# Five small edits to a block-sorted attention and cosine-gated MLP kernel: where one output tile, two transposes and the last columns live, and when one transpose and two value products run

## The chip, the cores and the metric

The kernel runs on one core of a Trainium2 chip. The core has a matrix engine (PE, with its weight loads listed apart as PEld), a vector engine (DVE), a scalar engine (ACT), a GpSimd engine (POOL) and a sync engine (SP), each with its own in-order instruction queue, and 16 DMA engines that all queues share. Matrix products land in PSUM, a small memory of eight banks per partition; DVE and ACT copy from there to SBUF, and DMAs move SBUF to and from device memory. The metric is the device time of one execution in microseconds (us); lower is better.

## The reference

```python
# attention: 4 batches x 8 heads, 768 tokens of 64, 8 blocks of 96 tokens
P = sort_net
for _ in range(5):
    P = exp(P - max(P, -1))
    P = P / (sum(P, -1) + 1e-9)
    P = P / (sum(P, -2) + 1e-9)
k_sorted = einsum('bhij,bhjcd->bhicd', P, k_blocks)
v_sorted = einsum('bhij,bhjcd->bhicd', P, v_blocks)
attn = softmax(q_block @ k_sorted_block.T / sqrt(64))
x = attn @ v_sorted_block            # -> 3072 tokens x 512
# MLP
h = x @ w_in                         # 512 -> 2048
out = (h * cos(h)) @ w_out           # 2048 -> 512, float32
```

Every query block of 96 tokens attends to one block of keys, which is a mixture of all eight key blocks of its head; the result goes through an MLP whose gate is the cosine of its own input.

## The kernel before

**Chunks.** The 3072 tokens are cut into eight chunks, n = 0 to 7, of four blocks (u = 0 to 3) of 96 tokens: 384 tokens, or three output tiles of 128 tokens (ts = 0 to 2). For each chunk the kernel makes scores (`qk`, `qk_half`; in the first two chunks `s_ps`, `s_max`, `s_sub`), exponentials on ACT (`expo`), the transpose of the exponentials (a DMA that SP issues, or PE products with an identity), the value products with their normalisation on DVE (`av` is `av_products` and then `av_norm`), and the transpose of the normalised tokens into `xT` (a DMA that SP issues, or `x_transpose` on PE with a copy from PSUM). The MLP follows: `up` makes two of sixteen column blocks of h in PSUM, ACT takes their cosine into a tile `c`, DVE multiplies both into `gg`; `down` sums sixteen products of 512 columns per output tile, in two halves of eight, and copies the sum to SBUF for the store.

**Order.** Nothing schedules the work: each engine runs its instructions in the order in which the program writes them (`manual_schedule`). A `moe_down` call takes lists of attention steps for a later chunk: list e runs after the e-th of six halves (`slots`), and `mid={e: ...}` runs between the fourth and the fifth product of half e. So the attention of chunk n + 1 is threaded by hand through the MLP of chunk n. An instruction that waits holds all that is written behind it on its engine.

**Buffers.** A tile pool hands out its buffers in turn; a new tile waits until the readers of the buffer's previous tile are done. The pools that matter here:

```python
cosp = ctx.enter_context(tc.tile_pool(name="cosp", bufs=2))
op = ctx.enter_context(tc.tile_pool(name="op", bufs=2))
big = ctx.enter_context(tc.tile_pool(name="big", bufs=3, space=bass.MemoryType.PSUM))
acc = ctx.enter_context(tc.tile_pool(name="acc", bufs=2, space=bass.MemoryType.PSUM))
```

`big` has three PSUM buffers of two banks and `acc` two of one bank; the program calls them `B` and `C` (line 618). `cosp` holds the cosines and `op` the output tiles in SBUF that wait for their store. From chunk 3 on most output tiles go to parts of the old value buffer instead (`vbuf`, the first half of the tile `kv`), six places of 512 float32 columns, and are stored one chunk later (`let_go`).

**The places that the change and the prediction touch.**

- End of chunk 0 and of the attention of chunk 1 (lines 940 to 984): `down_out(2, A)` (line 950) copies chunk 0's third output tile by ACT to an `op` buffer; its two buffers were taken by the other two output tiles. Behind it ACT copies one token transpose and four products of the key mixing (`kse` for 3, 2, 1 and 0; the fifth, 5, is DVE's). Then come `k_swap(kT[1])` (line 968, two DMAs on SP that bring key halves to the other partitions, behind the last of the `kse`), the query transposes `q_transpose(2, 0)` and `(2, 1)` (969, 970; sixteen PE products each, placed by DVE), `up(1, 0)` (977), two groups of value mixing (`v_sort_b`), `up(1, 1)`, and `qk_half(2, 0, 0)` (984), the first products that read the swapped keys.
- End of chunk 1 (lines 1021 to 1027): value products of chunk 2 and its token transposes `x_transpose(2, u)`, each into a `big` buffer, among the halves of the third output tile.
- `moe_down(3)` (line 1060): the last list runs `av(4, 3)`, `expo(5, 0)`, the transpose of tokens of blocks 1 and 2 together, and `qk(5, 1)`.
- `moe_down(6)` (line 1088): `av(7, 2)` behind the third half, `av(7, 3)` behind the fourth.
- The tail (lines 1095 to 1109): the last output tile in two halves of 256 columns, each with sixteen products into `acc`; the second half is copied by DVE and ACT, 128 columns each, into one `op` tile, and stored by two DMAs, of SP and of ACT.

Of the kernel before, what the change touches and what calls it, by code (L numbers as in the profile page):

```python
# [10 lines left out]
FP32 = mybir.dt.float32  # L11
# [7 lines left out]
def kernel(  # L19
# [15 lines left out]
    nc = tc.nc  # L35
    B, H, S, D = q.shape
# [3 lines left out]
    Ntok, Dm = out.shape  # L40
# [9 lines left out]
    TC = IC * blk  # L50
    KC = Dm // 128
    FC = Dff // 128
# [8 lines left out]
    cosp = ctx.enter_context(tc.tile_pool(name="cosp", bufs=2))  # L61
    gp = ctx.enter_context(tc.tile_pool(name="gp", bufs=5))
    op = ctx.enter_context(tc.tile_pool(name="op", bufs=2))
    ctx.enter_context(tc.manual_schedule())

    big = ctx.enter_context(tc.tile_pool(name="big", bufs=3, space=bass.MemoryType.PSUM))
    acc = ctx.enter_context(tc.tile_pool(name="acc", bufs=2, space=bass.MemoryType.PSUM))

    kv = const.tile([128, 2 * CD], BF16, name="kv")
    vbuf, kbuf = kv[:, :CD], kv[:, CD:]  # L70
# [11 lines left out]
                      in_=sort_net.rearrange("b h i j -> (b h) (i j)"))  # L82
# [71 lines left out]
    w_out_t = const.tile([128, FC, Dm], BF16, name="w_out_t")  # L154
# [90 lines left out]
    V, A = nc.vector, nc.scalar  # L245

    def copy_on(eng, dst, src):
        if eng is nc.scalar:
            eng.copy(dst, src)  # L249
        else:  # L250
            eng.tensor_copy(dst, src)
# [3 lines left out]
    def q_products(n, z, lo, hi, pool, tag):  # L255
        if lo == 0:
            q_ps[n, z] = pool.tile([128, 2, IC, QR, blk // QR], BF16, name="qps", tag=tag)
        for i in range(lo, hi):
            e, hp, r = i // (2 * QR), i // QR % 2, i % QR
            nc.tensor.transpose(  # L260
                q_ps[n, z][hp * D:(hp + 1) * D, e, :, r],
                q_rows[:, (z * 2 + e) * 2 + hp, r * D:(r + 1) * D], ident[:blk, :blk])

    def q_transpose(n, z, engs, pool, tag):
        q_products(n, z, 0, 4 * QR, pool, tag)
        for hp, eng in enumerate(engs):
            q_place_half(n, z, hp, eng)

    def q_place_half(n, z, hp, eng):
        rows = slice(hp * D, (hp + 1) * D)  # L270
        dst = q_of(n, hp)[rows, :QW].rearrange("d (i h c) -> d h i c", h=H2, c=blk)
        copy_on(eng, dst[:, z * 2:z * 2 + 2],
                q_ps[n, z][rows].rearrange("d e i r p -> d e i (r p)"))
# [263 lines left out]
    def x_transpose(n, u, eng, pool, tag, to=None):  # L537
        us = range(u, (u if to is None else to) + 1)
        ps = pool.tile([128, KC, len(us), blk], BF16, name="xps", tag=tag)

        turn = order[:] if n < NQ else ident[:blk, :blk]
        for i, z in enumerate(us):
            xn = xn_t.pop((n, z))
            for h2 in range(H2):
                nc.tensor.transpose(  # L545
                    ps[:, h2, i], xn[:, h2].rearrange("p e d -> p (e d)"), turn)
        copy_on(eng, xT[n][:, :, u * blk:us.stop * blk], ps.rearrange("p k i c -> p k (i c)"))

    gt = {}
# [21 lines left out]
    def store(n, ts, o_s, eng=nc.sync):  # L571
        r0 = n * TC + ts * 128
        eng.dma_start(out=out[r0:r0 + 128, :], in_=o_s[:])
# [4 lines left out]
    def down(n, ts, half, stores, mid=()):  # L578
        if half == 0:
            out_ps[ts] = acc.tile([128, Dm], FP32, name="o", tag="acc")  # L580
        o = out_ps[ts]
        for f in range(half * FC // 2, (half + 1) * FC // 2):
            nc.tensor.matmul(  # L583
                o[:], gt[n, f // 4][:, f % 4, ts * 128:(ts + 1) * 128], w_out_t[:, f, :],
                start=(f == 0), stop=(f == FC - 1))
            if f % (FC // 2) == FC // 4 - 1:
                step(mid)
        if half == 0:
            return
        if stores is None:  # L590

            z = (n % 2 * 3 + ts) * 2 * Dm
            o_s = vbuf[:, z:z + 2 * Dm].bitcast(FP32)
        else:
            o_s = op.tile([128, Dm], FP32, name="o_s", tag="o_s")
        late = n > 0 and ts == TC // 128 - 1
        copy_on(V if late else A, o_s[:], o[:])
        if stores is None or stores == "held":
            kept[n, ts] = o_s
        else:  # L600
            store(n, ts, o_s, nc.sync if late else stores)

    def step(calls):
        for f, *args in calls:
            f(*args)
# [6 lines left out]
    def moe_down(n, slots=(), stores=nc.sync, mid={}):  # L612

        for e in range(2 * TC // 128):
            down(n, e // 2, e % 2, stores, mid.get(e, ()))
            step(slots[e] if e < len(slots) else ())

    B, C = (big, "big"), (acc, "acc")
# [139 lines left out]
                start=(f == 0), stop=(f == FC - 1))  # L758

    def down_out(ts, eng):  # L760
        o_s = op.tile([128, Dm], FP32, name="o_s", tag="o_s")
        copy_on(eng, o_s[:], out_ps[ts][:])
        store(0, ts, o_s)

# [201 lines left out]
    kse(5, V)  # L966
    kse(0, A)
    k_swap(kT[1])
    q_transpose(2, 0, (V, V), *B)
    q_transpose(2, 1, (V, V), *B)  # L970
    zeros_between(3)
    load_q(3)
# [50 lines left out]
    av(2, 2, True)  # L1023
    x_transpose(2, 1, V, *B)
    av(2, 3, True)
    x_transpose(2, 0, V, *B)
    down(1, 2, 1, nc.sync, mid=[(k_sort_g, 20, A, *B), (x_transpose, 2, 2, V, *B), (x_transpose, 2, 3, V, *B)])
    q_transpose_dma(4)
    moe_up(2, [[(k_next,), (qk_half, 3, 0, 0)], [(k_next,)],
# [4 lines left out]
    def ahead(n, *more):  # L1034
# [5 lines left out]
        for e, calls in more:  # L1040
# [8 lines left out]
             mid={5: [(x_transpose, 3, 1, V, *B), (x_transpose, 3, 2, V, *B),  # L1049
                  (x_transpose, 3, 3, V, *B)]})  # L1050
# [9 lines left out]
    moe_down(3, [[(qk, 4, 3), (expo, 4, 2)], [(w_next, A, *B), (qk, 5, 0), (expo, 4, 3)],  # L1060
                 [(av, 4, 0)],
                 [(av, 4, 1, True), (av, 4, 2, True)],
                 [(av, 4, 3, True), (expo, 5, 0), (x_transpose, 4, 1, A, *B, 2), (qk, 5, 1)]],
             None, mid={5: [(x_transpose, 4, 3, A, *B)]})

    q_transpose_dma(6)
# [8 lines left out]
             None, mid={3: [(av, 5, 1)], 5: [(x_transpose, 5, 3, A, *B)]})  # L1075
# [7 lines left out]
             mid={5: [(x_transpose, 6, 3, A, *B)]})  # L1083
# [1 line left out]
               [(qk_half, 7, 3, 1)]])  # L1085
    expo(7, 2)
    expo(7, 3)
    moe_down(6, [[(av, 7, 0)], [(av, 7, 1)], [(av, 7, 2, True)], [(av, 7, 3, True)],
                 [(x_transpose, 7, 2, A, *B)]], None,
             mid={5: [(x_transpose, 7, 3, A, *B)]})  # L1090
    moe_up(7, [[(let_go, 6, 0)], [(let_go, 6, 1)], [(let_go, 6, 2)]])
    for e in range(2 * TC // 128 - 2):
        down(7, e // 2, e % 2, nc.sync)

    ts, w = TC // 128 - 1, Dm // 2
    for z in range(2):
        o = acc.tile([128, w], FP32, name="o", tag="acc")
        for f in range(FC):
            nc.tensor.matmul(
                o[:], gt[7, f // 4][:, f % 4, ts * 128:(ts + 1) * 128],  # L1100
                w_out_t[:, f, z * w:(z + 1) * w], start=(f == 0), stop=(f == FC - 1))
        o_s = op.tile([128, w], FP32, name="o_s", tag="o_s")
        for e, (eng, dma) in enumerate((((A, nc.scalar),), ((V, nc.sync), (A, nc.scalar)))[z]):
            c = slice(e * w // 2, (e + 1) * w // 2) if z else slice(0, w)
            copy_on(eng, o_s[:, c], o[:, c])
            dma.dma_start(
                out=out[7 * TC + ts * 128:8 * TC, z * w:(z + 1) * w][:, c], in_=o_s[:, c])

# [1 line left out]
_INS = ['q', 'k', 'v', 'sort_net', 'moe_w_in', 'moe_w_out']  # L1110
# [26 lines left out]
```

## Time and profile before

| | |
|---|---|
| median of three runs | 241.41 us (241.0 to 241.5) |
| the profiled execution's own time | 240.86 us |
| its span, first to last instruction | 239.1 us |
| granted TensorE clock over the span | 1.000 |
| PE busy / weight loads busy | 227.4 us / 143.9 us |
| DVE / ACT / POOL busy | 171.1 / 153.9 / 93.6 us |
| bytes moved by DMA, mean rate | 30.89 MB, 129 GB/s |

The profiled execution is 0.55 us shorter than the median; between its span and its time lie 1.76 us. How to read the lines below: a row of the timeline has the start in us, the length, the engine, the line in the program, the operation with output <- input, shapes, a count where neighbouring rows were merged, and in brackets how long the engine stood idle before it and what seemed to end that. PE products overlap in the pipeline, so a row's length includes about 0.17 us of drain that the next row does not wait for. In the chain of waits the overlap is taken out: its lengths add up. "DMA to landing" is the time from the issue of a DMA on its queue until its semaphore tells that the data is there.

### The profile page before, as it was taken

The numbers are of one execution on the slowest core, as the hardware profiler recorded it, in microseconds if no ns is written. First come the engines' busy times: TensorE is split into PE (matmuls) and PEld (weight loads), VectorE is DVE, ScalarE is ACT, GpSimd is POOL, SyncE is SP. The second block draws the span as 40 slices with busy tenths as digits, with TensorE's granted clock in tenths as the row PEclk, the third lists the DMA queues.
The fourth block names the chain that finished last, engine by engine and source line by source line (L and its number), as shares of the span: only waits on it lengthen the run. The fifth ranks groups of instructions, "written<-read, shape, count | busy, mean of one in ns | idle before, by whom it ended". The sixth has DMA issues, their size and how long they took to land.

```text
span 239.1 us, 5377 instructions
## 1 busy us (share of the span) xinstructions
PE 227.4 (95%) x2191; PEld 143.9 (60%) x2214; DVE 171.1 (72%) x284; ACT 153.9 (64%) x205; POOL 93.6 (39%) x117
## 2 busy tenths in 40 slices
PE   8789999998999989999999989999999999999993
PEld 2468799566765656656666556655565565455552
DVE  5658976886789666893689966998698869535700
ACT  3357966586889747896688737674666477546511
POOL 7689994893970098930808005300000000000000
PEclk9999999999999999999999999999999999999999
DMA  6999999895899989769889959934973450341012
GB/s 87 210 201 204 205 221 216 142 194 159 102 108 190 144 154 140 141 154 187 102 93 109 122 103 238 79 60 88 127 205 57 84 174 3 66 121 47 0 44 88
DMA packets 66423, 30.89 MB, mean 129 GB/s; under 512 B 55136, under 2 KB 61920, under 8 KB 66144
## 3 DMA queue, kind: packets, MB, share of 16 engines
q0 software_dynamic: 24048, 13.64, 41.7%
q1 hardware_dynamic: 42064, 16.73, 32.8%
q8 instruction: 17, 0.28, 0.5%
q10 hardware_dynamic: 288, 0.20, 0.3%
q14 instruction: 6, 0.05, 0.1%
HBM read 27.27 MB, written 6.29 MB: 140 GB/s over the span
## 4 chain that ended last, share of the span: by engine, by line
PE 81%; DMA 6%; ACT 5%; DVE 3%; issue 3%; POOL 1%; SPq 0%; ACTq 0%; POOLq 0%
PE h L558 31%; PE o L583 22%; PE h L735 4%; PE o L756 4%; PE sc L405 3%; DMA pT<-p_buf 3%; PE av L514 3%; PE vs L662 2%; PE ks L375 2%; PE vs L425 1%; ACT p_buf L467 1%; DMA vperm<-p_buf 1%; PE pps L713 1%; DMA xT<-xn 1%; PE xps L545 1%
## 5 line engine op out<-in xcount | busy, mean ns | idle before, releaser
L558 PE MATMUL h<-xT,w_in_t 128*128 128x384 bf16 x448 | 78.4, 326 | 0.2 <-DMA xT<-xn 0.2
L583 PE MATMUL o<-w_out_t,gg 128*128 128x512 bf16 x303 | 73.6, 379 | 0.9
L566 DVE TENSOR_TENSOR gg<-c,h 128x768 bf16<-128x768 f32 x56 | 52.6, 949 | 19.0 <-ACT c L562 19.0
L562 ACT ACTIVATE c<-h,half_pi 128x768 f32<-128x768 f32 x56 | 50.4, 900 | 22.2 <-PE h L558 21.3
L558 PEld LDWEIGHTS <-w_in_t 128*128 128x128 bf16 x448 | 42.2, 98 | 26.5 <-issue 0.6
L583 PEld LDWEIGHTS <-gg 128*128 128x128 bf16 x320 | 29.1, 98 | 27.6
L179 POOL COPY vperm<-kv 64x1536 bf16<-64x1536 bf16 (+1 forms) x10 | 28.0, 2849 | 1.1 <-DMA kv<-in_v_dram 1.1
L467 ACT ACTIVATE p_buf<-s 96x768 bf16<-96x768 f32 x32 | 26.0, 840 | 3.0 <-DVE s L702 2.4
L449 DVE TENSOR_TENSOR s<-sc,mx 96x384 f32<-96x384 f32 (+1 forms) x33 | 24.3, 735 | 1.8
L447 DVE TENSOR_REDUCE mx<-sc 96x4 f32<-96x384 f32 (+1 forms) x33 | 24.0, 728 | 0.7 <-PE sc L405 0.7
L527 DVE TENSOR_TENSOR xn<-av,r 96x512 bf16<-96x512 f32 x32 | 22.0, 686 | 1.1
L525 DVE RECIPROCAL r<-av 96x8 f32<-96x8 f32 x32 | 6.3, 198 | 14.8 <-PE av L514 14.6
L129 POOL DMA_DIRECT2D kv<-in_q_dram x24 | 16.0, 681 | 0.8 <-issue 0.8
L405 PE MATMUL sc<-kTs,q_turned 128*128 128x96 bf16 x224 | 15.3, 206 | 0.0
L249 ACT CAST kTs<-ks 128x512 bf16<-128x512 f32 (+1 forms) x18 | 10.9, 637 | 6.4 <-PE ks L375 6.4
L405 PEld LDWEIGHTS <-q_turned 128*128 128x128 bf16 x224 | 12.7, 98 | 3.8 <-DVE s L449 0.4
L249 ACT COPY kv<-o 128x512 f32<-128x512 f32 x8 | 4.7, 582 | 12.8 <-PE o L583 12.8
L249 ACT COPY o_s<-o 128x512 f32<-128x512 f32 (+2 forms) x10 | 5.3, 532 | 10.7 <-PE o L583 6.4
L756 PE MATMUL o<-w_out_t,gg 128*128 128x512 bf16 x45 | 11.2, 380 | 0.2
L129 POOL DMA_DIRECT2D q_mem<-in_q_dram x16 | 10.7, 691 | 1.3 <-DMA kv<-in_v_dram 1.0
L735 PE MATMUL h<-xT,w_in_t 128*128 128x192 bf16 x128 | 11.1, 246 | 0.0
L238 PE MATMUL idle<-warm 128*128 128x512 bf16 x28 | 8.7, 450 | 2.4 <-ACT q_turned L321 1.4
(118 smaller groups left out, 282.8 us busy)
## 6 DMA issues: line engine op xcount, KB each, us to landing
out_dram<-kv SPq DMA_DIRECT2D x12, 256.0 KB, 2.5
out_dram<-o_s SPq DMA_DIRECT2D x11, 256.0 KB, 3.2
w_in_t<-in_moe_w_in_dram POOLq DMA_DIRECT2D x4, 512.0 KB, 12.2
w_out_t<-in_moe_w_out_dram POOLq DMA_DIRECT2D x4, 512.0 KB, 12.8
kv<-in_k_dram POOLq DMA_DIRECT2D x2, 768.0 KB, 10.2
kv<-in_v_dram POOLq DMA_DIRECT2D x2, 768.0 KB, 13.3
pair<-in_k_dram POOLq DMA_DIRECT2D x2, 768.0 KB, 11.3
kv<-in_v_dram POOLq DMA_DIRECT2D x6, 256.0 KB, 5.4
```

Of the source, the lines that this page charges most:

```text
L129: nc.gpsimd.dma_start(out=q_heads[:, i, :, e], in_=src[:, ih * IC + i, :, e])
L179: nc.gpsimd.tensor_copy(dst, src)
L249: eng.copy(dst, src)
L405: nc.tensor.matmul(out, q_of(n, hp)[:, x:x + 128], keys_of(n, u, h2, hp), start=True, stop=True)
L447: nc.vector.reduce_max(mx[:], scv, axis=AX.X)
L449: nc.vector.tensor_tensor(s, scv, mx.to_broadcast(list(s.shape)), op=ALU.subtract)
L467: nc.scalar.activation(p[:, :, :blk], s_t.pop((n, u)).rearrange("p e h c -> p (e h) c"), AF.Exp, scale=scale)
L527: nc.vector.tensor_tensor(xn.rearrange("p h e d -> p e h d"), avv[:, :, :, :D], r.to_broadcast([blk, 2, H2, D]), op=ALU.mult)
L558: nc.tensor.matmul(h[:, f2, :w], w_in_t[:, kk, f * 128:(f + 1) * 128], xT[n][:, kk], start=(kk == 0), stop=(kk == KC - 1))
L562: nc.scalar.activation(c[:], h[:, :, :w], AF.Sin, bias=half_pi[:, 0:1])
L566: nc.vector.tensor_tensor(gt[n, fp // 2][:, f:f + 2], c[:], h[:, :, :w], op=ALU.mult)
L583: nc.tensor.matmul(o[:], gt[n, f // 4][:, f % 4, ts * 128:(ts + 1) * 128], w_out_t[:, f, :], start=(f == 0), stop=(f == FC - 1))
```

## The change

1. `down_out`: the third output tile of chunk 0 goes to a buffer of the cosine pool, of which it uses 512 of 768 columns, instead of an `op` buffer.
2. `q_transpose(2, 0)` and `x_transpose(2, 0)` take `acc` buffers instead of `big` buffers.
3. `moe_down(3)`, last list: the transpose of blocks 1 and 2 comes first, then `expo(5, 0)`, then `av(4, 3)`, then `qk(5, 1)`.
4. `moe_down(6)`: `av(7, 2)` runs in the middle of the fourth half instead of ahead of it.
5. The tail: the last columns are 256, 128 and 128, each with its own `big` tile; the two tiles of 128 take turns, product by product. The copies go to the last place of `vbuf` instead of `op` tiles.

```diff
     def down_out(ts, eng):
-        o_s = op.tile([128, Dm], FP32, name="o_s", tag="o_s")
+        if ts < 2:
+            o_s = op.tile([128, Dm], FP32, name="o_s", tag="o_s")
+        else:
+            o_s = cosp.tile([128, 2, TC], FP32, name="c", tag="c")
+            o_s = o_s.rearrange("p b c -> p (b c)")[:, :Dm]
         copy_on(eng, o_s[:], out_ps[ts][:])
         store(0, ts, o_s)
...
-    q_transpose(2, 0, (V, V), *B)
+    q_transpose(2, 0, (V, V), *C)
     q_transpose(2, 1, (V, V), *B)
...
-    x_transpose(2, 0, V, *B)
+    x_transpose(2, 0, V, *C)
...
-                 [(av, 4, 3, True), (expo, 5, 0), (x_transpose, 4, 1, A, *B, 2), (qk, 5, 1)]],
+                 [(x_transpose, 4, 1, A, *B, 2), (expo, 5, 0), (av, 4, 3, True), (qk, 5, 1)]],
...
-    moe_down(6, [[(av, 7, 0)], [(av, 7, 1)], [(av, 7, 2, True)], [(av, 7, 3, True)],
+    moe_down(6, [[(av, 7, 0)], [(av, 7, 1)], [], [(av, 7, 3, True)],
                  [(x_transpose, 7, 2, A, *B)]], None,
-             mid={5: [(x_transpose, 7, 3, A, *B)]})
+             mid={3: [(av, 7, 2, True)], 5: [(x_transpose, 7, 3, A, *B)]})
...
-    ts, w = TC // 128 - 1, Dm // 2
-    for z in range(2):
-        o = acc.tile([128, w], FP32, name="o", tag="acc")
+    ts = TC // 128 - 1
+    for parts in (((0, 256, A, nc.scalar),), ((256, 128, V, nc.sync), (384, 128, A, nc.scalar))):
+        tiles = [big.tile([128, w], FP32, name="o", tag="big") for _, w, *_ in parts]
         for f in range(FC):
-            nc.tensor.matmul(
-                o[:], gt[7, f // 4][:, f % 4, ts * 128:(ts + 1) * 128],
-                w_out_t[:, f, z * w:(z + 1) * w], start=(f == 0), stop=(f == FC - 1))
-        o_s = op.tile([128, w], FP32, name="o_s", tag="o_s")
-        for e, (eng, dma) in enumerate((((A, nc.scalar),), ((V, nc.sync), (A, nc.scalar)))[z]):
-            c = slice(e * w // 2, (e + 1) * w // 2) if z else slice(0, w)
-            copy_on(eng, o_s[:, c], o[:, c])
-            dma.dma_start(
-                out=out[7 * TC + ts * 128:8 * TC, z * w:(z + 1) * w][:, c], in_=o_s[:, c])
+            for o, (c, w, *_) in zip(tiles, parts):
+                nc.tensor.matmul(
+                    o[:], gt[7, f // 4][:, f % 4, ts * 128:(ts + 1) * 128],
+                    w_out_t[:, f, c:c + w], start=(f == 0), stop=(f == FC - 1))
+        for o, (c, w, eng, dma) in zip(tiles, parts):
+            o_s = vbuf[:, (5 * Dm + c) * 2:(5 * Dm + c + w) * 2].bitcast(FP32)
+            copy_on(eng, o_s, o[:])
+            dma.dma_start(out=out[7 * TC + ts * 128:8 * TC, c:c + w], in_=o_s)
```

What it does to the instructions, at three places on ACT. The rows are the engine's instructions in order, with the semaphores each waits for: PE, DVE, Activation and Pool are the engines' own, DMAHW and DMASW those of DMAs issued by hardware queues and by POOL.

The first is the end of chunk 0, where ACT copies the third output tile (`o_1078`); the `xT` and `kTs` copies behind it belong to chunk 1's tokens and to the key mixing.

```order
 L249 COPY xT_1035<-xps_1109 128x4x96 [waits PE_49]
 L249 COPY pT_1095<-pps_1114 96x768 [waits PE_49]
-L249 COPY o_s_1155<-o_1078 128x512 [waits DMAHW1_49,PE_49,Activation_49]
+L249 COPY c_1155<-o_1078 128x512 [waits PE_49]
 L249 COPY xT_1035<-xps_1158 128x4x96 [waits PE_49]
 L249 COPY kTs_98<-ks_1167 128x2x32x8 [waits PE_49]
```

The copy keeps its place and no longer waits for a DMA.

The second is the last list of `moe_down(3)`: the copy of the joint token transpose of chunk 4 (`xps`, 192 columns) and the exponential of chunk 5's first block (`p_buf2_108`).

```order
 L467 ACTIVATE p_buf1_107<-s_2347 96x8x96 [waits DMAHW4_49,DVE_49]
 L249 COPY kv_87<-o_2394 128x512 [waits DMASW5_49,PE_49]
+L249 COPY xT_2403<-xps_2462 128x4x192 [waits PE_49]
 L467 ACTIVATE p_buf2_108<-s_2378 96x8x96 [waits DMAHW5_49,DVE_49]
-L249 COPY xT_2403<-xps_2477 128x4x192 [waits PE_49]
 L249 COPY xT_2403<-xps_2504 128x4x96 [waits PE_49]
 L562 ACT_TABLE_LOAD
```

The copy moved ahead of the exponential; on PE its eight products moved ahead of the value products of `av(4, 3)` in the same way.

The third is ACT's end: the copies of the last 256 and 128 columns and their DMAs.

```order
 L249 COPY o_s_3474<-o_3457 128x512 [waits PE_49]
 L249 COPY o_s_3494<-o_3477 128x512 [waits PE_49]
-L249 COPY o_s_3514<-o_3497 128x256 [waits DMAHW5_49,PE_49,Activation_49]
-L1106 DMA out_0_dram<-o_s_3514 128x256 [waits DMAHW7_49,Activation_49]
-L249 COPY o_s_3534<-o_3517 128x128 [waits DMAHW6_49,DVE_49]
-L1106 DMA out_0_dram<-o_s_3534 128x128 [waits DMAHW1_49,Activation_49]
-L1132 UNCONDITIONAL_BRANCH
+L249 COPY kv_87<-o_3497 128x256 [waits DMAHW5_49,DMASW6_49,PE_49]
+L1110 DMA out_0_dram<-kv_87 128x256 [waits DMAHW7_49,Activation_49]
+L249 COPY kv_87<-o_3517 128x128 [waits PE_49]
+L1110 DMA out_0_dram<-kv_87 128x128 [waits DMAHW0_49,Activation_49]
```

The last copy waited for DVE, which copies the other half of the same tile, and for a DMA; it now waits for PE alone.

## The prediction

> **What bounds the kernel now.** I read the page first.
>
> ```profile
> span 239.1 us, 5377 instructions
> PE 227.4 (95%) x2191; PEld 143.9 (60%) x2214; DVE 171.1 (72%) x284; ACT 153.9 (64%) x205; POOL 93.6 (39%) x117
> PE 81%; DMA 6%; ACT 5%; DVE 3%; issue 3%; POOL 1%; SPq 0%; ACTq 0%; POOLq 0%
> ```
>
> PE is busy nearly throughout, and four fifths of the chain that ends last are its products. The change adds none but sixteen small ones at the end, so it can only win where PE stands still. I therefore read the timeline and the chain at the five places of the change.
>
> **Place 1, end of chunk 0.** The rows are the timeline's; the three last lines are landing times, of the store issued at 49.21 (it carries the first `op` buffer), of the two key-swap DMAs here, and of the next such pair, at 100.32 and 100.84.
>
> ```profile
> 49.21 9.13 SPq L573 DMA_DIRECT2D out_dram<-o_s  x3
> 55.32 0.80 ACT L249 COPY pT<-pps 96x768 bf16<-96x768 bf16 x1
> 55.53 0.86 PE o L756 x4
> 56.92 0.69 DVE L527 TENSOR_TENSOR xn<-av,r 96x512 bf16<-96x512 f32 x1
> 57.40 0.58 ACT L249 COPY o_s<-o 128x512 f32<-128x512 f32 x1 [1.28 <-PE xps L722]
> 58.04 0.39 PE L375 MATMUL ks<-bd,kv 128*128 128x64 bf16 x8 [0.70 <-ACT o_s L249]
> 58.25 2.08 ACT L249 CAST kTs<-ks 128x512 bf16<-128x512 f32 x4
> 59.89 0.88 PE L260 MATMUL qps<-ident,q_mem 96*64 96x96 bf16 x32 [0.30 <-ACT kTs L249]
> 60.94 0.59 SPq L389 DMA_DIRECT2D kTs<-kTs  x1
> 64.12 0.33 PE L405 MATMUL sc<-kTs,q_turned 128*128 128x96 bf16 x4
> DMA to landing us min/median/max: 8.1/8.1/8.1
> 60.47 2.31 DVE L251 COPY q_turned<-qps 64x768 bf16<-64x768 bf16 x4 [0.44 <-PE qps L260]
> DMA to landing us min/median/max: 2.8/2.9/3.0
> DMA to landing us min/median/max: 3.7/4.4/5.0
> ```
>
> ACT's copy of the third tile could start when its sum is done, 55.53 + 0.86 = 56.39, and ACT is free from 56.12. It starts at 57.40. The row blames PE's `xps`, but the copy also waits for a DMA, and the store lands at 49.21 + 8.1 = 57.31: that is the wait. Behind it on ACT stand the four `kTs` casts, and PE waits for these twice (0.70, 0.30).
>
> With a cosine buffer the copy starts at about 56.42, 0.98 earlier. The ACT queue follows if its inputs come in time. The fourth is the tightest: its products need the token transpose after DVE's `xn` (56.92 + 0.69 = 57.61), then DVE's copy of that transpose (to about 58.40) and the last eight products (0.39 in the row at 58.04, done at 58.85), so the last cast ends near 59.40 instead of 60.33. The swap DMAs wait for it: the second goes out at 60.01 instead of 60.94 and lands at 60.01 + 3.0 = 63.01 instead of 63.94. The scores that read it start at about 63.07 instead of 64.12: **1.05 us**.
>
> The query turn in the other pool removes PE's wait of 0.30 for a cast, and lets the two turns run while casts are still going on. With both edits PE reaches `up(1, 0)` 1.24 us earlier, but then waits about 0.2 at the scores for the swap. The turn alone, without the first edit, would win almost nothing for that reason; I give it nothing of its own. It adds a wait: the second `v_sort_b` now needs DVE's placing of that turn. Four placings take 2.31; the two of this turn, behind DVE's last cast (to 59.2 by the same steps), end at 60.4, and PE gets there at 61.1. Cover 0.7. Bounds of the sum of both: 1.24 if the swap lands a little sooner; 0.1 if it takes a microsecond more (the next pair took up to 5.0).
>
> **Place 2, chunk 2's token transpose.**
>
> ```profile
> 85.96 0.69 DVE L527 TENSOR_TENSOR xn<-av,r 96x512 bf16<-96x512 f32 x1
> 86.71 0.34 PE L545 MATMUL xps<-order,xn 96*128 96x96 bf16 x4 [0.59 <-DVE xn L527]
> 87.06 0.69 DVE L527 TENSOR_TENSOR xn<-av,r 96x512 bf16<-96x512 f32 x1
> 87.97 0.51 PE L545 MATMUL xps<-order,xn 96*128 96x96 bf16 x8
> ```
>
> The third `big` buffer is held until DVE's `xn` at 86.65, so PE loses 0.59. In `acc` the buffer has been free since ACT's `pT` copy, and the transpose runs at 85.95. But the last transpose of the group needs the second `xn`, 87.06 + 0.69 = 87.75, whatever PE does before. It can run at 87.80 to 87.97; today both run in one row and end at 87.97 + 0.51 less the drain of 0.17, 88.31. So **0.33 us**, not 0.59; bounds 0.2 and 0.59.
>
> **Place 3, `moe_down(3)`.**
>
> ```profile
> 136.53 4.51 DMA pT<-p_buf
> 138.28 1.89 PE L583 MATMUL o<-w_out_t,gg 128*128 128x512 bf16 x8
> 139.15 0.69 DVE L527 TENSOR_TENSOR xn<-av,r 96x512 bf16<-96x512 f32 x1
> 139.38 1.63 SPq L480 DMA_TRANSPOSE vperm<-p_buf  x1
> 141.09 0.43 PE L514 MATMUL av<-pair,pT 96*128 96x65 bf16 x8 [0.91 <-DMA pT<-p_buf]
> 141.35 0.51 PE L545 MATMUL xps<-ident,xn 96*128 96x96 bf16 x8
> 132.48 2.80 DMA pT<-p_buf
> 141.70 3.59 SPq L149 DMA_TRANSPOSE q_turned<-q_mem  x2
> 156.91 0.34 PE sc L405 x8
> 158.97 0.26 PE av L514 x8
> ```
>
> PE is through with the half at about 140.01 and waits to 141.09 for the exponentials' transpose. The token transpose moved ahead needs `xn`, done at 139.84, so its eight products (0.34) fill part of the wait: **0.34 us**. The chain's row at 132.48 has a DMA of the same kind that took 2.80, this one took 4.51; if it landed after 2.80, at 139.3, the whole 1.08 would go. I take 0.34, since nothing ahead of it in its queue changes; the transpose at 139.38, which moves, stands behind it. Bounds 0.34 and 1.08.
>
> The exponential moves behind the copy on ACT, from 138.29 to about 141.3. Its DMA goes out at 142.2 instead of 139.38, and the query transposes behind it on SP (141.70) and the stores behind those slip by some 2 us; GpSimd's next load of queries waits for the transposes and slips too. The readers come at 156.91 (scores) and 158.97 (value products). Even if issue and landing together took 3.59 + 4.51, the transposes would be there by 152. No cost; without that slack of 5 us it would be up to 2.
>
> **Place 4, `moe_down(6)`.**
>
> ```profile
> 206.10 1.89 PE L583 MATMUL o<-w_out_t,gg 128*128 128x512 bf16 x8
> 208.24 0.43 PE L514 MATMUL av<-pair,vperm 96*128 96x65 bf16 x8 [0.25 <-DMA vperm<-p_buf]
> ```
>
> Eight products take 1.73 without drain, so PE is free at 207.83 and waits 0.41 for the DMA. Four products (0.86) put in between hide it wholly: **0.41 us**; bounds 0.3 and 0.41. The normalised tokens are then needed by a transpose more than 2 us later.
>
> **Place 5, the tail.**
>
> ```profile
> 231.77 1.76 PE o L1099 x16
> 235.35 0.29 DVE L251 COPY o_s<-o 128x128 f32<-128x128 f32 x1 [8.57 <-PE o L1099]
> 235.68 0.27 ACT L249 COPY o_s<-o 128x128 f32<-128x128 f32 x1 [1.71 <-DMA out_dram<-o_s]
> 235.97 0.34 ACTq L1106 DMA_DIRECT2D out_dram<-o_s  x1
> 108.18 0.45 PE vs L425 x8
> L1099 PEld LDWEIGHTS <-gg 128*128 128x128 bf16 x32 | 3.1, 97 | 0.6
> ```
>
> ACT's copy starts when DVE's ends (235.64). With a tile each they run side by side, and the last DMA goes out 0.29 earlier. The products become 32 of 128 columns: eight such, with a weight load each, took 0.45, so 32 take 1.80 instead of 1.76. Net **0.26 us**; bounds 0 (if SP's DMA ends last anyway) and 0.29. The Trainium skill, "TensorE: Matmul & The Clock Gate", section "Back-to-back issue gap", says that a stream of weight loads and 128-column products sustains about 81 ns per product. That would be 2.59 us, 0.83 more, an estimate; the trace disagrees with it at 0.45 / 8 = 56 ns, and I go by the trace.
>
> **The sum.** 1.05 + 0.33 + 0.34 + 0.41 + 0.26 = 2.39 us. The profiled execution would go from 240.86 to 238.47. The median lies 0.55 above that execution, so I expect 241.41 - 2.39 = **239.0 us**, a gain of 1.0%. The five places follow one another on PE, so gains add as long as no DMA in between is tied to something that does not move; the loads I followed are all released by transposes or exponentials that shift along.
>
> **Rivals.**
>
> The slow transpose of place 3 lands sooner: 0.74 more, 238.3 us. For it: the 2.80 at 132.48. Against: the order in its queue is the same.
>
> The swap or a load holds chunk 2: place 1 wins only 0.1, and the time is 240.0 us. For it: the next pair's 5.0. Against: this pair took 3.0, and what shares the engines with it shifts along.
>
> Weight loads show in the tail: a load takes 97 ns, and 32 of them unhidden 3.10 us instead of 1.76, so the tail loses 1.08 and the time is 240.4. Against: the 56 ns above. By the skill's figure it would be 239.9.
>
> The slower side: the cosine pool has two buffers, and the third tile takes one until its store lands. The second cosine of chunk 1 (`up(1, 1)`) needs it at about 62.9 after the shift; behind it on ACT stand all evictions of the stage. The store goes out at 57.05, so a landing up to 5.9 us is free. Beyond that each microsecond costs nearly one, and from about 8.3 us the whole change loses.
>
> ```profile
> DMA to landing us min/median/max: 3.8/3.8/3.8
> ```
>
> That is today's store of this tile; the first took 8.1. At 8.1 the stall is 2.2 and the time about 241.2; at 10 it is 243. Against it: the big loads that the first store shared the engines with are over by 57.
>
> The change does nothing: other waits refill the holes, 241.4 us.
>
> **Chances.** Forecast 0.56; sooner transpose 0.14; swap 0.14; tail 0.04; store 0.05; nothing 0.07. 0.2%, about what a measurement of this kernel can tell from no change, is 0.5 us. The first four are faster, 0.88; of "nothing" I give 0.03 to faster and 0.04 to the same; the store is slower. So faster 0.91, same 0.04, slower 0.05. All high bounds give 3.61 us, 237.8; the swap's rival gives 240.0, and the low bounds of other terms a little more. Range 237.8 to 240.2.
>
> **What the profile would show.** Right: the third tile's copy within 0.1 us of its sum's end; PE's waits of 0.70, 0.30 and 0.59 gone; a short wait at the first scores of chunk 2; the joint transpose ahead of the value products in `moe_down(3)` with some 0.7 of wait left; no wait at `av(7, 2)`; both last copies starting together. Wrong: a cosine of chunk 1 released by a store, 81 ns per product in the tail, or chunk 2 starting at its old time.

## The result, and the profile after

The changed kernel took 238.77 us in the median of four runs (238.38 to 239.64), the kernel before on the same chip 241.45 (four runs, 241.0 to 242.54): a ratio of 0.9887 [0.9845, 0.993]. A second comparison, with 7 runs of the changed kernel and 30 of the one before, gave 0.9934 [0.9899, 0.9969]. The change makes the kernel faster, by 0.7 to 1.1%. The forecast, 239.0 us or a ratio of 0.990, lies in both intervals, in the second at its very edge. As will be seen, the largest term of the sum nevertheless rested on one sample of a time that changes from execution to execution.

The first lines of the page of the changed kernel, to set beside those of before:

```profile
span 236.9 us, 5429 instructions
PE 228.3 (96%) x2230; PEld 144.0 (61%) x2230; DVE 171.1 (72%) x284; ACT 154.0 (65%) x205; POOL 93.4 (39%) x117
PE 81%; DMA 6%; ACT 4%; DVE 4%; issue 3%; POOL 1%; SPq 0%; ACTq 0%; POOLq 0%
```

PE's busy time did not fall (227.4, then 228.3 us), and the span is 2.2 us shorter: what went away is standing still. To find where, compare the start of chunk 2's first scores (`sc`) and the first product of each `up` in the two timelines (in us):

| mark | before | after | gained since the mark above | predicted |
|---|---|---|---|---|
| first scores of chunk 2 | 64.12 | 63.18 | 0.94 (place 1) | 1.05 |
| `up(2, 0)` | 89.18 | 87.91 | 0.33 (place 2) | 0.33 |
| `up(3, 0)` | 116.45 | 115.54 | -0.36 (no edit here) | 0 |
| `up(4, 0)` | 143.94 | 142.54 | 0.49 (place 3) | 0.34 |
| `up(5, 0)` | 167.95 | 166.55 | 0 | 0 |
| `up(6, 0)` | 191.39 | 189.97 | 0.02 | 0 |
| `up(7, 0)` | 214.30 | 212.45 | 0.43 (place 4) | 0.41 |
| end of the span | 239.1 | 236.9 | 0.35 (place 5) | 0.26 |

The rows behind these, from the timeline of the changed kernel. Place 1:

```profile
56.42 0.59 ACT L249 COPY c<-o 128x512 f32<-128x512 f32 x1 [0.31 <-PE o L756]
57.34 2.12 ACT L249 CAST kTs<-ks 128x512 bf16<-128x512 f32 x4
58.77 0.90 PE L260 MATMUL qps<-ident,q_mem 96*64 96x96 bf16 x32
59.60 1.47 PE L558 MATMUL h<-xT,w_in_t 128*128 128x384 bf16 x8
60.08 0.59 SPq L389 DMA_DIRECT2D kTs<-kTs  x1
62.93 0.90 ACT L562 ACTIVATE c<-h,half_pi 128x768 f32<-128x768 f32 x1
63.18 0.33 PE L405 MATMUL sc<-kTs,q_turned 128*128 128x96 bf16 x4
```

The third tile's copy now names PE's sum as what it waited for, and starts at 56.42 instead of 57.40. The casts, the second swap DMA (60.94 to 60.08) and the scores (64.12 to 63.18) follow it. The second cosine of chunk 1 (62.93) has no wait in brackets: the store in the cosine buffer, out at 57.03, landed after 2.4 us.

Places 2, 3 and 4, and the unforeseen loss between them:

```profile
86.87 0.34 PE L545 MATMUL xps<-order,xn 96*128 96x96 bf16 x4 [0.27 <-DVE xn L527]
87.91 1.30 PE L558 MATMUL h<-xT,w_in_t 128*128 128x384 bf16 x7
108.13 0.84 ACT L467 ACTIVATE p_buf<-s 96x768 bf16<-96x768 f32 x1 [1.47 <-DMA pT<-p_buf]
109.94 0.61 PE L425 MATMUL vs<-bd,vperm 128*128 128x128 bf16 x8 [0.34 <-ACT pair L249]
139.12 0.51 PE L545 MATMUL xps<-ident,xn 96*128 96x96 bf16 x8
140.03 0.43 PE L514 MATMUL av<-pair,pT 96*128 96x65 bf16 x8 [0.41 <-DMA pT<-p_buf]
207.27 0.42 PE L514 MATMUL av<-pair,vperm 96*128 96x65 bf16 x8
```

At 86.87 the second transpose waits for `xn`, as said, for 0.27 where 0.59 was waited before. At 139.12 the joint transpose stands ahead of the value products, and 0.41 is left of their wait of 0.91. At 207.27 nothing is left. At 108.13 ACT waits 1.47 for a transpose of exponentials, and at 109.94 PE waits 0.34 for what ACT does behind it. The transpose that ACT waited for was issued at 103.71. These are its landing time in the changed kernel and that of the same transpose, issued at 104.99, in the kernel before:

```profile
DMA to landing us min/median/max: 4.3/4.3/4.3
DMA to landing us min/median/max: 2.9/2.9/2.9
```

The chain of waits of the changed kernel gives the lateness of the transpose behind 140.03 (the median of the kind is 3.0):

```profile
135.62 4.37 DMA pT<-p_buf
...
229.92 3.55 PE o L1104 x48
```

Its second row is the tail's 48 products. The copies behind them, from the timeline:

```profile
231.70 0.37 ACT L249 COPY kv<-o 128x256 f32<-128x256 f32 x1 [1.16 <-PE o L1104]
233.43 0.29 DVE L251 COPY kv<-o 128x128 f32<-128x128 f32 x1 [8.50 <-PE o L1104]
233.49 0.27 ACT L249 COPY kv<-o 128x128 f32<-128x128 f32 x1 [1.41 <-PE o L1104]
233.78 0.34 ACTq L1110 DMA_DIRECT2D out_dram<-kv  x1
```

Both last copies wait for PE alone and start 0.06 apart, one product. ACT's first copy waits for the end of the sixteen products of 256 columns, its last for the end of the 32 of 128 columns: 233.49 - 231.70 = 1.79 us, 56 ns per product.

### The profile page after: what moved, and what is told of

Same layout as the page of the kernel before. It is cut to its first block, busy times and chain, and to the rows that moved or that the text cites. A ratio compares the mean times of both kernels' runs of the same rounds, so it can differ in the third digit from the quotient of the medians.

```text
span 236.9 us, 5429 instructions
## 1 busy us (share of the span) xinstructions
PE 228.3 (96%) x2230; PEld 144.0 (61%) x2230; DVE 171.1 (72%) x284; ACT 154.0 (65%) x205; POOL 93.4 (39%) x117
## 4 chain that ended last, share of the span: by engine, by line
PE 81%; DMA 6%; ACT 4%; DVE 4%; issue 3%; POOL 1%; SPq 0%; ACTq 0%; POOLq 0%
PE h L558 31%; PE o L583 21%; DMA pT<-p_buf 5%; PE h L735 5%; PE o L756 4%; PE sc L405 3%; PE av L514 3%; PE ks L375 2%; PE vs L662 2%; ACT p_buf L467 2%; PE o L1104 1%; PE vs L425 1%; PE pps L713 1%; DMA xT<-xn 1%; PE vs L238 1%
## 5 line engine op out<-in xcount | busy, mean ns | idle before, releaser
L583 PE MATMUL o<-w_out_t,gg 128*128 128x512 bf16 x320 | 76.5, 379 | 0.0
L249 ACT COPY kv<-o 128x512 f32<-128x512 f32 (+2 forms) x10 | 5.3, 530 | 14.9 <-PE o L583 12.4
L756 PE MATMUL o<-w_out_t,gg 128*128 128x512 bf16 x48 | 11.4, 379 | 0.0
L251 DVE COPY kv<-o 128x512 f32<-128x512 f32 (+1 forms) x5 | 3.0, 602 | 11.4 <-PE o L1104 8.5
```

The costliest lines, as they stand in the source:

```text
L583: nc.tensor.matmul(o[:], gt[n, f // 4][:, f % 4, ts * 128:(ts + 1) * 128], w_out_t[:, f, :], start=(f == 0), stop=(f == FC - 1))
```

## The experiments

The first eight of these kernels were timed once each, so their times tell little under 1 us; they are read by their rows. The kernel before took 241.84 us beside the first four and 240.84 beside the next four.

### One edit at a time

**The cosine tile alone.**

```diff
 # in the kernel before
+        if ts < 2: o_s = op.tile(...)
+        else:      o_s = cosp.tile([128, 2, TC], ...)
```

> The kernel before with the first edit alone: chunk 0's third output tile in a cosine buffer. Theory: ACT's copy of that tile starts within 0.1 us of its sum's end (56.4 instead of 57.4), the four casts and the key swap behind it move by the same 0.9 to 1.0 us, and the first scores of chunk 2 start at 63.2 instead of 64.1, because they wait for the swap and not for PE. So this edit alone carries all of place 1: span 238.1 to 238.4 against 239.1. Rival, that the query turn in the other pool carries a share: first scores no earlier than 63.5, span 238.6 or more.

Measured: 240.12 us. The copy started at 56.42 and the scores at 63.20, so the tile alone does what all of place 1 does in the changed kernel (63.18).

**The query turn alone.**

```diff
-    q_transpose(2, 0, (V, V), *B)
+    q_transpose(2, 0, (V, V), *C)
```

> The kernel before with chunk 2's first query turn in the other pool and nothing else. Theory: PE no longer waits 0.30 us for a cast and reaches up(1, 0) 0.3 to 0.5 us earlier, but the swap still goes out at 60.94 and lands near 63.9, so the scores start at 64.0 to 64.1 as before and the span stays at 239.0 to 239.2. Rival, that the turn is worth what PE no longer waits: scores at 63.7, span 238.7.

Measured: 241.32 us. In the timeline:

```profile
57.00 0.59 ACT L249 COPY o_s<-o 128x512 f32<-128x512 f32 x1 [0.89 <-PE xps L722]
63.62 0.33 PE L405 MATMUL sc<-kTs,q_turned 128*128 128x96 bf16 x4 [0.19 <-DMA kTs<-kTs]
```

The scores start 6.62 behind the copy (before: 6.72), and they wait for the swap. The turn is worth 0.1 at most; the scores come near the rival's 63.7 because the copy started 0.40 earlier. The first of the two rows shows this, and it is a surprise: the copy has the `op` tile here, as before, and starts at 57.00, not at 57.40.

**The list of `moe_down(3)` alone.**

```diff
-  [(av, 4, 3, True), (expo, 5, 0), (x_transpose, 4, 1, A, *B, 2), (qk, 5, 1)]
+  [(x_transpose, 4, 1, A, *B, 2), (expo, 5, 0), (av, 4, 3, True), (qk, 5, 1)]
```

> The kernel before with the last list of moe_down(3) in its new order and nothing else. Theory: the wait for the exponentials' transpose stays where it is and the eight token products fill 0.34 us of it; the transpose lands 4.3 to 4.6 us after its issue as before, so chunk 4's first MLP product starts 0.3 to 0.5 us earlier and the span is 238.6 to 238.8. Rival, that the moved exponential had kept the transpose from landing: it lands after 2.8 to 3.0 us, and the span is 238.0 to 238.2.

Measured: 241.16 us. Chain and timeline:

```profile
137.22 4.47 DMA pT<-p_buf
```

```profile
57.95 0.59 ACT L249 COPY o_s<-o 128x512 f32<-128x512 f32 x1 [1.84 <-DMA out_dram<-o_s]
141.73 0.43 PE L514 MATMUL av<-pair,pT 96*128 96x65 bf16 x8 [0.52 <-DMA pT<-p_buf]
```

The slow transpose stays slow (4.47), so the rival of a sooner landing falls, and a wait of 0.52 is left. From `up(3, 0)` to `up(4, 0)` it is 27.10 us. Here the copy at the end of chunk 0 starts later than before, at 57.95, and this time the row names the DMA; so the span, 239.4, misses the 238.6 to 238.8 that were expected.

**The tail alone.**

```diff
 # in the kernel before: the last 256 columns as two tiles of 128
+    for parts in (((0, 256, ...),), ((256, 128, V, ...), (384, 128, A, ...))):
```

> The kernel before with the new tail alone: three tiles of 256, 128 and 128 columns, and copies to the value buffer. Theory: the 32 products of 128 columns take 1.75 to 1.85 us, both last copies start within 0.1 us of each other, and the last DMA goes out 0.26 to 0.35 us earlier in the span: 238.75 to 238.85. Rival, that weight loads show behind 128-column products (81 to 97 ns each): 2.6 to 3.1 us for the 32, and a span of 239.6 to 240.1.

Measured: 240.01 us. In the timeline:

```profile
56.49 0.59 ACT L249 COPY o_s<-o 128x512 f32<-128x512 f32 x1 [0.39 <-PE o L756]
233.03 0.37 ACT L249 COPY kv<-o 128x256 f32<-128x256 f32 x1 [1.16 <-PE o L1100]
234.77 0.29 DVE L251 COPY kv<-o 128x128 f32<-128x128 f32 x1 [8.50 <-PE o L1100]
234.82 0.27 ACT L249 COPY kv<-o 128x128 f32<-128x128 f32 x1 [1.41 <-PE o L1100]
```

From `up(7, 0)` to the end it is 24.46 us instead of 24.79; the 32 products again take 1.79 (233.03 to 234.82). The first row says more: with no edit there, the copy of chunk 0's third tile waits for PE only and starts at 56.49, almost as with the cosine tile. The wait that place 1 removes was almost gone in this execution, and the span, 238.2, is shorter than the tail alone can make it.

### The changed kernel with one thing different

**The query turn back in `big`.**

```diff
-    q_transpose(2, 0, (V, V), *C)
+    q_transpose(2, 0, (V, V), *B)
```

> The changed kernel with chunk 2's first query turn back in the larger pool. Theory: the scores of chunk 2 wait for the key swap, so the turn is worth nothing with the other edits either: PE reaches up(1, 0) at about 59.8 instead of 59.6, the scores start at 63.1 to 63.3 and the span is 236.8 to 237.0, as with it. Rival: scores at 63.5 or later, span 237.2 or more.

Measured: 238.75 us, scores at 63.20 (changed kernel 63.18). The turn is worth nothing.

**The first scores of chunk 2 later**, to see whether the swap bounds place 1.

```diff
-    qk_half(2, 0, 0, *C)
 ...  # up(1, 2) and the value mixing behind it
+    qk_half(2, 0, 0, *C)
```

> The changed kernel with the first half of chunk 2's first scores one group of MLP products later (behind up(1, 2) and its value mixing). Theory: if the swap is the bound at 63.18, PE now goes on with up(1, 2) at about 63.0 and the swap has landed long before the scores, so the stage ends 0.15 to 0.3 us earlier (up(2, 0) at 87.7 to 87.9 instead of 88.08). Rival, that PE was not held by the swap: no change within 0.05 us.

Measured: 239.42 us. In the timeline:

```profile
62.92 1.47 PE L558 MATMUL h<-xT,w_in_t 128*128 128x384 bf16 x8
64.46 0.33 PE L405 MATMUL sc<-kTs,q_turned 128*128 128x96 bf16 x4
67.42 0.34 PE L405 MATMUL sc<-kTs,q_turned 128*128 128x96 bf16 x4 [1.10 <-DVE s L449]
```

The third `up` pair starts at 62.92. In the changed kernel the scores start at 63.18 and that pair at 63.34, 0.42 later; the scores' four products are 0.17 of it, so 0.25 is what the swap had held. The gain that was expected did not show in the total, because the second half of the scores came too soon behind the first and waited 1.10 for DVE to free the `acc` buffer; `up(2, 0)` starts at 88.93 instead of 87.91 (the expectation's 88.08 is the second product of the same `up`). So the swap was the bound, and a later bound took more than it had.

**The third tile's store later**, behind the key swap on SP: the slower rival's mechanism.

```diff
-        store(0, ts, o_s)
+        if ts < 2: store(0, ts, o_s)
+        else:      kept[0, ts] = o_s
 ...
     k_swap(kT[1])
+    let_go(0, 2)
```

> The changed kernel with the store of chunk 0's third tile put behind the key swap on SP, some 3.6 us later than in the changed kernel (about 60.7 instead of 57.03). This takes away the slack that hid the slower side of the prediction: the second cosine of chunk 1 wants the tile's buffer at 62.93. Theory: with a landing of 2 to 4 us the store ends at 62.7 to 64.7, ACT's cosine waits up to 1.8 us for it, PE loses less than that, and the span is 236.9 to 238.5. If the cosine starts at 62.9 to 63.0 with no DMA named before it, the store landed in time and the slack is larger than was reckoned.

Measured: 239.95 us. In the timeline:

```profile
60.72 0.59 SPq L573 DMA_DIRECT2D out_dram<-c  x1
63.65 0.33 PE L405 MATMUL sc<-kTs,q_turned 128*128 128x96 bf16 x4 [0.55 <-DMA kTs<-kTs]
64.25 0.90 ACT L562 ACTIVATE c<-h,half_pi 128x768 f32<-128x768 f32 x1 [1.26 <-DMA out_dram<-c]
```

The store landed 3.4 us after 60.72, the second cosine waited 1.26 for it, and `up(2, 0)` started at 88.99, 1.08 late. The rival's mechanism exists. In the changed kernel it has 62.93 - 57.03 = 5.9 us, of which the landing took 2.4.

**A fourth place for exponentials**, so that `expo(3, 3)` need not wait for the late transpose (the loss of 0.36).

```diff
-        p = p_bufs[cnt[0] % NP]
-        cnt[0] += 1
+        if (n, u) == (3, 3): p = vbuf[...]     # an unused place
+        else:                p = p_bufs[cnt[0] % NP]; cnt[0] += 1
```

> The changed kernel with a buffer of its own for the exponentials of chunk 3's last block (an unused place of the value buffer), so that they no longer wait for the transpose that reads one of the three buffers. Theory: in the changed kernel these exponentials waited 1.47 us for a transpose that landed 3.85 us after its issue, and PE lost 0.36 us behind the cast on ACT; without the buffer's wait PE's value mixing starts with no idle time before it and up(3, 0) starts at 115.3 to 115.4 instead of 115.70, unless the value products then wait for the late transpose itself. Rival, that the late landing holds the value products anyway: no change of more than 0.1 us.

Measured: 240.04 us. ACT's wait of 1.47 is gone, but `up(3, 0)` starts at 115.38, only 0.16 earlier (115.54 in the changed kernel; the expectation's 115.70 is its second product), and then over 1 us is lost. The wait had been for the transpose issued at 103.71, which landed after 4.3; the 3.85 of the expectation belongs to the next one. In the timeline of this kernel:

```profile
112.19 0.43 PE L517 MATMUL av<-vS,pT 96*128 96x65 bf16 x8 [0.16 <-DMA pT<-kv]
116.92 1.28 ACT L565 ACT_TABLE_LOAD   x1 [2.80 <-PE h L561]
119.65 0.38 PE L425 MATMUL vs<-bd,vperm 128*128 128x128 bf16 x4 [1.11 <-ACT pair L249]
```

and of the changed kernel:

```profile
114.31 1.28 ACT L562 ACT_TABLE_LOAD   x1
```

The load of ACT's table for the next cosine stood idle until PE had made the first `h`, and so came 2.6 us later, in front of the cosine instead of in a hole. ACT's instructions in order show why. With the fourth place:

```
 L565 ACT_TABLE_LOAD [waits PE_49]
 L565 ACTIVATE c<-h,half_pi 128x768 [waits Activation_49]
```

In the changed kernel the load waits for nothing and the cosine has the wait on PE. With the fourth place the cosine has two semaphores to wait for, and one of the two was put on the instruction ahead of it; which dependence asks for the second stays open. So the late transpose did cost something at this place: PE's idle time of 0.34 behind ACT is gone, and the value products wait 0.16 for their own transpose instead. But what removed it cost more elsewhere.

### Timed comparisons

These ran on one chip with five rounds and shared 30 runs of the kernel before (median 240.92 us).

**The cosine tile alone, timed.** The edit is that of the first experiment.

> The first edit alone again, now timed in rounds against the kernel before. In ten profiles so far the store of the first output tile landed 6.9 to 8.6 us after its issue, and ACT's copy of the third tile could have started at 56.42. Theory: the edit is worth what the store lands later than that, 0 to 1.5 us from one execution to the next, and 0.5 us (0.2%) in the mean of the ten. Rival, that the 1.05 us read from the one profile is what it is worth on the whole: 0.4%.

Measured: 240.45 us (12 runs, 239.91 to 242.06), ratio 0.9994 [0.9967, 1.002]. The tile alone makes no difference that these runs can tell. The rival's 1.05 us would be a ratio of 0.9956, outside this interval; the expected 0.5 us (0.998) is inside it, and so is nothing.

**The changed kernel without the cosine tile.**

```diff
-        if ts < 2: o_s = op.tile(...)
-        else:      o_s = cosp.tile(...)
+        o_s = op.tile([128, Dm], FP32, name="o_s", tag="o_s")
```

> The changed kernel with chunk 0's third output tile back in the output pool, all other edits kept. Theory: 1.5 to 1.9 us (0.6 to 0.8%) faster than before, that is 0.3 to 0.7 us slower than the changed kernel in the same rounds; in the profile the copy of the third tile starts when the store lands (49.2 plus the landing time) or at 56.4, whichever is later. Rival: 1.05 us slower than the changed kernel.

Measured: 239.37 us (12 runs, 238.43 to 242.09), ratio 0.993 [0.99, 0.9961]. Beside the changed kernel's 239.25 us (next run) that is 0.1 slower, not 0.3 to 0.7 as expected, and not the rival's 1.05. Its profiled copy of the third tile started by PE's sum, without the cosine tile:

```profile
56.46 0.58 ACT L249 COPY o_s<-o 128x512 f32<-128x512 f32 x1 [0.36 <-PE o L756]
```

**The changed kernel again**, with nothing different.

> The changed kernel again, timed on the same chip as the two above. Theory: 2.0 to 2.6 us (0.85 to 1.1%) faster than before; in its profile the first scores of chunk 2 start at 63.1 to 63.3 whatever the first store's landing time, while the later stages move by up to 0.6 us with the landing times of the transposes.

Measured: 239.25 us (7 runs, 238.24 to 240.89), ratio 0.9934 [0.9899, 0.9969], the same as without the tile. The gain is 1.6 us, less than the 2.0 to 2.6 expected. The scores start at 63.18, as expected. One stage of its profiled execution, `up(3, 0)` to `up(4, 0)`, was with 28.14 us a microsecond longer than in the changed kernel's first profile (27.00), where up to 0.6 had been expected. The timeline shows two waits for transposes, which landed after 5.0 and 4.6 us:

```profile
137.94 0.43 PE L514 MATMUL av<-pair,pT 96*128 96x65 bf16 x8 [1.05 <-DMA pT<-p_buf]
138.87 0.43 PE L514 MATMUL av<-pair,pT 96*128 96x65 bf16 x8 [0.50 <-DMA pT<-p_buf]
```

**One of the late transposes on PE instead of a DMA**, to remove what is left of the wait at place 3 and look for a faster version.

```diff
-   [(w_next, A, *B), (qk, 5, 0), (expo, 4, 3)]
+   [(w_next, A, *B), (qk, 5, 0), (expo, 4, 3, True)]
...
-   [(av, 4, 1, True), (av, 4, 2, True)]
+   [(av, 4, 1, True), (av, 4, 2, True), (p_transpose, 4, 3, A, *B)]
```

> The changed kernel with the exponentials of chunk 4's last block turned on PE (eight products and a copy by ACT) instead of by a DMA, behind the value products of blocks 1 and 2 in moe_down(3). Theory: the turn costs PE 0.36 us and takes away the rest of the wait at those value products (0.74 us in the changed kernel's profile), so up(4, 0) starts about 0.2 us earlier than in the changed kernel against the same stage's start, and it no longer moves with the landing. Rival, that ACT's extra copy (0.80 us) delays the token copies behind it: no gain or a loss of up to 0.5 us.

Measured: 240.76 us (12 runs, 240.08 to 242.37), ratio 1.0004 [0.9973, 1.0035]: the whole gain of the change is given back, 1.5 us against the changed kernel beside it, where the rival had allowed 0.5. In the timeline:

```profile
139.62 0.42 PE L514 MATMUL av<-pair,pT 96*128 96x65 bf16 x8
167.08 4.06 PE L558 MATMUL h<-xT,w_in_t 128*128 128x384 bf16 x24 [1.12 <-DMA xT<-xn]
185.56 0.43 PE L514 MATMUL av<-pair,vperm 96*128 96x65 bf16 x8 [1.55 <-DMA vperm<-p_buf]
```

At the place itself it did what was expected: the value products wait for nothing, and `up(3, 0)` to `up(4, 0)` took 26.78 us instead of 27.00. The next two stages took 24.96 and 25.05 instead of 24.01 and 23.42, with waits for other transposes of chunks 5 and 6. Their place in the order was not changed: the token transpose that ended the wait of 1.12 went out 21.55 us behind `up(4, 0)`, 21.56 in the changed kernel, and landed after 3.3 us here, 2.3 there. The last section shows what went along with this. No version found here beats the changed kernel.

## Why the prediction was right, and where it was not

**The mechanism of place 1 held step by step.** The copy waited for the first store, not for PE's `xps` that the row names: with the cosine tile it starts at 56.42, to the hundredth what was worked out. The second swap went out at 60.08 (worked out: 60.01), the scores started at 63.18 (63.07), and what was gained in this pair of profiles is 0.94 of 1.05. The swap is the bound behind it: the scores start 0.14 to 0.23 us after its second DMA landed (63.04 in the changed kernel) in all 14 profiles but the one that moved them, the turn alone shows the wait, and the later scores show 0.25 of it for the changed kernel, whose own row at 63.18 names no wait. Only PE's arrival at `up(1, 0)` was off, 1.10 earlier and not 1.24, which cost nothing in front of that bound. The turn is worth nothing, with the tile (63.20 to 63.18) and without it (0.1 at most).

**Its size was the mistake.** The term of 1.05 came from one landing, 8.1 us. That store goes out at 49.2 in every kernel here, ahead of all edits, so each profiled execution is one more sample of it:

| profiled execution | landing, us | copy of the third tile |
|---|---|---|
| list alone | 8.6 | 57.95 |
| before | 8.1 | 57.40 |
| turn alone | 7.7 | 57.00 |
| tail alone | 7.2 | 56.49 |
| changed without the tile | 7.0 | 56.46 |
| the nine others, with the cosine tile | 6.9 to 8.0 | 56.42 to 56.44 |

The copy with an `op` tile starts about 0.1 behind the landing, and not ahead of PE's sum at 56.42. So the tile is worth what the landing exceeds 56.42 - 49.21 - 0.1 = 7.1 by. Over the 14 landings (8.1, 7.7, 8.6, 7.2, 7.4, 7.5, 8.0, 6.9, 7.1, 7.5, 7.7, 7.0, 7.1, 6.9) the mean of that is 0.41 us, and in five of them it is nothing. The profile of before was the second latest of 14. The timed runs allow this and rule out the 1.05: 0.9994 for the tile alone, and no difference between the change with it (0.9934) and without it (0.993), within intervals of 0.3%. They do not tell 0.41 from nothing.

**Place 2** was right in mechanism and size: 0.33 predicted and measured, with the second `xn` as the next bound. The sign "wait of 0.59 gone" said more than this working: 0.27 of a wait is left.

**Place 3**: the term was 0.34. This pair of profiles shows 0.49, but the stage `up(3, 0)` to `up(4, 0)` took 27.32 to 27.49 us in five profiles with the old order (mean 27.41) and 27.00 to 27.21 in six with the new (mean 27.12): 0.29. Three with the new order are left out: the fourth place for exponentials, the turn on PE, and the late one of 28.14. The last is the changed kernel itself; with it the new mean is 27.26 and the gain 0.14. Whether the new list has a part in such lateness, one profile cannot tell. That the slow transpose stays slow was right too (4.51, then 4.37 and 4.47; 4.3 to 4.6 in all 13 profiles that have it), and the exponential that moved back delayed nothing that PE shows.

**Place 4**: 0.41 predicted, 0.43 measured. From `up(6, 0)` to `up(7, 0)` it is 22.90 to 23.05 us in the six profiles with the old order and 22.48 to 22.60 in the eight with the new.

**Place 5**: 0.26 predicted, 0.35 measured. The products were right: 1.80 us worked out for the 32, 1.79 measured. (Among the rivals, the tail's loss of 1.08 takes off the net 0.26 where the 0.29 belongs; it should be 1.05, and the 239.9 behind it 239.8.) By the figure of the Trainium skill, "TensorE: Matmul & The Clock Gate", section "Back-to-back issue gap", the tail would have lost 0.8 us as an estimate; the traces of two kernels, with 56 ns per product in both, do not agree with it here. The mis-sized term is the 0.29 between the copies, which was DVE's copy by its length: from the start of one copy to the start of the other it was 235.68 - 235.35 = 0.33. The other 0.04 is that the first of the three tiles is copied 1.78 us behind its first product (229.92 in the chain of the changed kernel) and not 1.82 (231.77 to 233.59 before).

**What was not foreseen** is the loss of 0.36 in `moe_down(2)`, where no edit is: there, ACT held the stage behind a transpose that landed late, and PE stood idle for 0.34 of it. This comes and goes without the change: that transpose landed after 2.8 to 2.9 us in six profiles (before, the list alone, the tail alone, the turn back in `big`, the scores later, the store later) and after 4.1 to 4.7 in the other eight, the tile alone in both its profiles and the turn alone among them. PE's idle time behind ACT's cast is there in seven of these eight, 0.15 to 0.53, and in none of the six. In the eighth, the fourth place had removed it. The profile of before is one of the quick ones. The sum left room for a shift of this kind in the range, not as a term.

**The sum.** In the profiled pair, 0.94 + 0.33 - 0.36 + 0.49 + 0.02 + 0.43 + 0.35 = 2.2 us against 2.39. Over many executions, with 0.41 for place 1 and nothing for `moe_down(2)`, an estimate from the same terms is 0.41 + 0.33 + 0.29 + 0.43 + 0.35 = 1.8 us, a ratio of 0.9925 (1.7 us with the late stage of place 3 counted). It lies in both intervals, as the forecast's 0.990 does; the timed runs alone cannot tell the two apart, the 14 landings can. The forecast stayed close because the four smaller terms held and the loss on the largest is 0.6 us. That the first comparison gave 2.7 us, more than any of these sums, is luck as far as the runs tell: its interval reaches down to 1.7, and the second gave 1.6. Of the rivals, the sooner transpose fell and the weight loads fell. The store has its mechanism, but in the eight profiles that sent it out at 57.03 to 57.05 it landed after 2.2 to 4.6 us, so 1.3 us or more was to spare. A swap that lands a microsecond later was not seen: its second DMA landed after 2.95 or 2.96 us in 13 profiles and after 3.42 with the store behind it. Two transposes of `moe_down(3)` that landed late did cost a microsecond in one profile: a case that no rival named.

## What to carry to other kernels

A wait for a DMA in one profile is one sample of a landing time: before it is priced, look for the same transfer in other executions (any kernel that is unchanged up to there will do), and price its excess over the next bound, not the wait. Some such waits turn out to be steady, as those of places 3 and 4 did; only the other executions tell which. Waits for instructions on the engines (place 2, the two copies of place 5) came out within 0.04 of their rows and could be priced from one profile. A wait removed on an engine that is not the bound can hand its lateness on, to a buffer two instructions later (the scores) or to a table load in front (the fourth place), so read what the next bound is before spending on it.

## What the runs showed of the hardware beyond what was expected

- The same store, issued at 49.20 to 49.22 in all 14 executions, landed after 6.9 to 8.6 us, after the same ACT copy at 48.58 to 48.61. In 13 of them it landed 0.2 to 0.4 us behind a load of 768 KB of keys that POOL had issued at 43.6 and that took some 12 to 14 us; in the fourteenth (the turn back in `big`) 0.5 ahead of it. So the scatter of place 1 goes with that of the load; why the load varies is open. The third tile's store, 8 us later, landed after 2.2 to 4.6.
- An ACT table load can take over one of the semaphore waits of the activation behind it. Here it then ran at 116.92 instead of 114.31, no longer hidden, and PE waited 1.11 for what followed.
- Products of 128 columns, each with a weight load of its own, followed one another every 56 ns over 32 of them.

One more thing goes along with the late transposes. Of the 33 DMA transposes of exponentials and tokens in an execution (32 with the turn on PE), 8 to 14 landed after more than 3.05 us (up to 5.0); some are the same in every execution, others are not. The page has a DMA queue with 17 packets of 16 KB in each execution:

```profile
q8 instruction: 17, 0.28, 0.5%
```

In the 14 traces, the 321 transposes of exponentials landed as follows:

| a `q8` packet starts, seen from the issue of the transpose | transposes | landed after, us |
|---|---|---|
| at no time from 0.7 us before to 3.2 after | 191 | 2.8 to 3.2 |
| 0.7 to 0.35 before | 6 | 3.2 to 3.5 |
| 0.35 before to 2.2 after | 58 | 3.7 to 4.6 |
| 2.2 to 3.2 after | 66 | 34 of them 2.8 to 3.1, 32 of them 4.1 to 5.0 |

The transpose of `moe_down(2)` issued at 103.71 is in the last row, with a packet 2.3 us behind it. In the late stage of the changed kernel's second profile a packet starts at 135.4, where the first profile has it at 137.9; with the turn on PE one starts at 164.5 instead of 167.7, ahead of the wait of 1.12. No run moved a packet alone, so it is not shown that the packets cause the lateness, and why they start elsewhere is open.
